# A state-space and SwiGLU kernel on one core: spectra stored in quarters of 64 channels, and some work of the chunk loop moved between engines

## The chip, the core and the metric

The kernel runs on one core of a Trainium2 chip. The core has TensorE for matmuls (PE, with its weight loads shown as PEld), VectorE (DVE), ScalarE (ACT), GpSimd (POOL) and SyncE (SP), which here only issues DMAs. All DMAs, whichever queue issued them, share 16 DMA engines. The metric is device microseconds of one execution; a kernel's time is the median of its runs.

## The reference

Two layers, each a state-space convolution and then a SwiGLU feed-forward block, both on a layer norm and with a residual. The sequence has 2048 steps, 512 channels (D) and 128 states per channel (N); the inner width is 1376.

```python
dt = jnp.exp(log_dt)[:, None]
logdA, dB = dt * (A_re + 1j * A_im), dt * (B_re + 1j * B_im)
P = jnp.exp(logdA[:, :, None] * l[None, None, :])
K = jnp.einsum("dn,dnl,dn->dl", Cc, P, dB).real        # a kernel of 2048 taps per channel
y = causal_convolution(u, K) + u * Dskip               # written with FFTs of length 4096
...
x = x + A(layernorm(x)); x = x + B(layernorm(x))       # twice, with the same weights
# B: (silu(x @ w_gate) * (x @ w_up)) @ w_down
```

So the work is: make K from the parameters, convolve, and do the feed-forward matmuls.

## The kernel before, in words

**The two parts.** The first part, to about 288 us, makes the kernel K and its spectra. The second, from about 360 us, runs the blocks of 512 steps (`ssm` for the convolution, `ffn` for the feed-forward), with a transition in between. In the second part Tile's scheduler orders the instructions; in the first the order on ScalarE, VectorE, TensorE and GpSimd is that of the program text (`manual_schedule`).

**Making K.** The 512 channels are cut into 8 chunks of 64 (`DC`). For a chunk, the 2048 taps are written as a product of two factors, 32 by 64 powers, per state and channel:
- `gen_turns` (L373) shifts and doubles phase angles on VectorE (L377 for the small tile xz, L380 and L384 for the large one) and clears one row with GpSimd (L386);
- `gen_trig` (L389) makes sines and cosines on ScalarE, first of xz (four activations of 320 elements a partition, L393 to L398), then of the large tile (three of 2048);
- `gen_exp` (L401) makes decays on ScalarE;
- `gen_e` (L426) and `gen_g` (L441) multiply these on VectorE to the factors re/im and g. At the last doubling of g (n = 16) the second half product goes to a tile acc (L461, L462), and a DMA on GpSimd's queue adds it into g (L463);
- `lags` (L476) is 128 small matmuls on TensorE that contract over the states.

**Spectra.** `spread_in` (L494) copies the lags' result to SBUF on ScalarE. `spread` (L497) writes that to DRAM (kdr) and reads it back in four DMAs (kt), which brings lags to partitions; both are issued by SP. `skip` (L487) adds the direct term Dskip into the first lag, on VectorE. `spectra` (L527) does 32 matmuls for two of the four frequency groups (q0 and q0 + 2), copies the results out of PSUM with four ScalarE activations (L544 to L546), stores half products to DRAM (wdr) from SP's queue and, when these have landed, adds the others to them with accumulating DMAs from GpSimd's queue (`store_w`, L524). wdr holds, for each half of the channels and each frequency group, 128 partitions of two parts (real, imaginary) of 256 channels; a chunk writes 64 channels of each part, 256 bytes in a row.

**Norms of the weights.** `norms` (L302) runs beside: GpSimd's queue loads blocks of the feed-forward weights (tiles st, three buffers), ScalarE squares them (L321), TensorE sums the squares (L324), VectorE takes the largest (L327). Three blocks make a group here. `second_block` adds 8 matmuls a part for the second block of the input (L287).

**The order.** Each step is entered in a list with a planned time (`at`), relative to the start t of its chunk (`starts`: 0, 31, 62, 93, then 28 apart); the list is sorted and the text runs in that order. The times have no other meaning: each engine does its instructions in this order and waits for what each needs. Around the change, in a chunk's turn: lags at t; `upper`, the square L417, at t + 0.2; the factors' first steps from t + 0.2; the copy L494 and the spread at t + 7.1; squares of a first group of weights at t + 8.0 and loads of the second at t + 8.1; decays from t + 8.3; the half product and its DMA at t + 12.2; turns of the chunk after next at t + 13.0; squares of the second group at t + 14.5; sines at t + 17.0; the direct term at t + 17.1; spectra at t + 17.5 (the first two groups) and in the next turn at 6.9 (the other two).

In the second part, for each frequency group VectorE multiplies input spectra u with w (L756), sums (L759) and combines the parts (L760, L761); u and w come from w0r in SBUF or from wdr and udr in DRAM.

Of the kernel before, what the change touches and what calls it, by code (L numbers as in the profile page):

```python
# [16 lines left out]
OP = mybir.AluOpType  # L17
# [18 lines left out]
NCH = D // DC  # L36
NA = 5
# [36 lines left out]
def kernel(ctx, tc, x, a_re, a_im, b_re, b_im, c_re, c_im, log_dt, d_skip,  # L74
# [48 lines left out]
    w0r = sb.tile([P, 2, 4, 2, HD], F32, name="w0r")  # L123
# [19 lines left out]
    wdr = dram.tile([NB, 2, 4, P, 2, HD], F32, name="wdr")  # L143
    udr = [dram.tile([NB - 1, 2, 4, P, 2, HD], F32, name=f"udr{i}") for i in range(NL)]
# [89 lines left out]

    def norm_x(n):
        rs, nb = row_stats(n, 4, 1.0, "stats", lambda r: tl([P, D], "junk", "t1", BF16))
        for c in range(4):
            A.activation(n[:, c], n[:, c], AF.Identity, scale=rs[:, c:c + 1], bias=nb[:, c:c + 1])

    def forward(n, h, eh):  # L240
# [13 lines left out]
        for i, q in enumerate(QORD):  # L254
# [9 lines left out]
            with tc.high_priority(offset=BOOST):  # L264
# [7 lines left out]
                u = tl([P, 2, HD], "u", "u")  # L272
                A.activation(u, pf, AF.Copy, scale=2.0 ** -16 if eh else 1.0)  # L273
# [7 lines left out]
    def direct(b, h, q, n, space=psml):  # L281
# [7 lines left out]
        u = tl([P, 2, HD], "u", "uu")  # L289
        A.activation(u, pf, AF.Copy)  # L290
# [82 lines left out]
    def gen_turns(ch, ts):  # L373
# [4 lines left out]
                        am.unsqueeze(2).to_broadcast([P, 5, DC]), OP.logical_shift_left)  # L378
        tu = im[:, 33:65].bitcast(I32)
# [61 lines left out]
    def gen_g(ch, ts, g):  # L441
# [12 lines left out]
        for n in (1, 2, 4, 8, 16):  # L454
# [5 lines left out]
            if n == 16 and 0 < ch < NCH - 1:  # L460
                tmp = tl([P, 2, 16, DC], "acc", ("gb", "ga")[ch % 2])  # L461
# [25 lines left out]
    def skip(ch, kt):  # L487

        k = kt[0:1, :, 0]
        V.tensor_tensor(k, k, dsk[:, ch * DC:(ch + 1) * DC].rearrange("p (g d) -> p g d", g=4), OP.add)  # L490
# [33 lines left out]
    def store_w(h, off, q, wo, eng=nc.sync, **add):  # L524
        eng.dma_start(wdr[1:, h, q, :, :, off:off + DC].rearrange("k p i d -> p i k d"), wo.rearrange("p i k g d -> p i k (g d)"), **add)

    def spectra(ch, kt, q0):  # L527


        h, off = ch // 4, (ch % 4) * DC  # L530
# [4 lines left out]
        if q0:  # L535
            wo = spare[0][:, 16 * DC:].rearrange("p (j i k g d) -> p j i k g d", j=2, i=2, k=NB - 1, g=4)
        else:
            wo = tl([P, 2, 2, NB - 1, 4, 16], "wo", "sg")
        wf = pw.rearrange("p j i k g d -> p j i k (g d)")
        wa = tl([P, 2, 2, NB - 1, 4, 16], "wa", "z")  # L540
        wv = wo.rearrange("p j i k g d -> p j i (k g d)")
        pv = pw.rearrange("p j i k g d -> p j i (k g d)")
        for i, sign in signs(q0):
            A.activation(wv[:, :, i], pv[:, :, 1 - i, :3 * DC], AF.Copy, scale=sign)  # L544
        A.activation(wa.rearrange("p j i k g d -> p j i (k g d)"), pv[:, :, :, DC:], AF.Copy)
# [695 lines left out]
```

## Time and profile before

| what | us |
|---|---|
| median of three runs | 1205.04 (1196.44 to 1207.28) |
| the profiled execution, its own time | 1204.58 |
| its span, first to last instruction | 1202.8 |
| set-up, to the first copy L494 at 69.30 | 69.3 |
| chunk loop, 69.30 to 288.21 | 218.9 |
| transition, to 360 | 71.8 |

A line of a profile's table gives where it stands: start and length for single instructions, or a group's busy time, mean and the idle time just before it with what ended that idle time. `[3.12 <-DMA kt<-kdr]` says: the engine had stood idle 3.12 us, and the last thing that it waited for was the DMA that fills kt from kdr. xN at the end of a row is a number of instructions. In the table by stretches (two times joined by a colon) each engine has its busy time and its number of instructions, and the last three columns are the granted clock of TensorE, the mean busy share of the DMA engines and GB/s.

### The profile page before, as it was taken

Reading aid. Unit: us, or ns where it says so; the run is one execution under the profiler, and the core shown is the slowest. Engines: PE = TensorE matmul, PEld = TensorE weight load, DVE = VectorE, ACT = ScalarE, POOL = GpSimd, SP = SyncE. Lnnn points to the kernel's source line nnn. Section 1 sums busy time; section 2 is a strip of 40 time slices with the busy share of each in tenths; the row PEclk is TensorE's granted clock in tenths of the full one; section 3 lists DMA queues with packets and bytes.
Section 4 is the critical chain, followed back from the end, with each engine's and each line's share of the span. In section 5 each row is a group of like instructions: output and inputs, shape, how many; then the busy total and the mean of one; then the engine's idle time right before and its main releaser. Section 6 shows DMA issues by size and latency. Waiting matters only on the chain.

```text
span 1202.8 us, 24436 instructions
## 1 busy us (share of the span) xinstructions
PE 1110.1 (92%) x9948; PEld 882.1 (73%) x9948; DVE 996.9 (83%) x1586; ACT 594.9 (49%) x1193; POOL 133.0 (11%) x176
## 2 busy tenths in 40 slices
PE   1978888998799999999999999999999998999998
PEld 1767777787687676878777686868687685867875
DVE  7998879685978999999899999999997999973211
ACT  6678777743283345356744253664533452234211
POOL 0013323332000010001110000010200000000000
PEclk9989999989999999999999999999999999999999
DMA  5368889989566337443324444342545145302000
GB/s 201 128 158 156 181 172 179 174 192 202 188 217 186 108 116 202 128 131 86 101 89 146 132 145 155 105 122 94 139 121 189 45 119 158 111 23 45 14 23 18
DMA packets 156915, 156.28 MB, mean 130 GB/s; under 512 B 95857, under 2 KB 104049, under 8 KB 156802
## 3 DMA queue, kind: packets, MB, share of 16 engines
q1 hardware_dynamic: 129314, 126.47, 35.0%
q0 software_dynamic: 27488, 28.25, 12.6%
q8 instruction: 78, 1.28, 0.4%
q14 instruction: 35, 0.29, 0.1%
HBM read 101.85 MB, written 36.57 MB: 115 GB/s over the span
## 4 chain that ended last, share of the span: by engine, by line
PE 33%; DVE 27%; issue 5%; DMA 4%; ACT 2%; SPq 1%; POOL 1%; DVEq 0%; POOLq 0%; ACTq 0%
PE pgu L888 6%; PE pgu L889 6%; PE pgu L891 6%; DVE t L756 5%; DVE yk L759 4%; PE py L903 3%; PE py L904 3%; PE py L905 3%; DMA mix<-nn 3%; DVE yk L756 2%; PE pi L775 2%; PE pf L271 2%; DVE z L227 2%; DVE hl L897 1%; DVE sg L895 1%
## 5 line engine op out<-in xcount | busy, mean ns | idle before, releaser
L888 PE MATMUL pgu<-mix,wsl 128*128 128x256 f16 x1280 | 298.9, 273 | 6.6 <-DVE xf L908 3.1
L889 PE MATMUL pgu<-mix,wsl 128*128 128x256 f16 x1280 | 298.8, 273 | 0.0
L891 PE MATMUL pgu<-mix,wsl 128*128 128x256 f16 x1280 | 193.9, 273 | 0.0
L889 PEld LDWEIGHTS <-wsl 128*128 128x128 f16 x1280 | 125.2, 98 | 23.6 <-issue 7.8
L903 PE MATMUL py<-wsl,hh 128*128 128x512 f16 (+1 forms) x352 | 134.1, 381 | 7.6 <-DVE xf L908 4.2
L888 PEld LDWEIGHTS <-wsl 128*128 128x128 f16 x1280 | 125.2, 98 | 15.9
L891 PEld LDWEIGHTS <-wsl 128*128 128x128 f16 x1280 | 125.3, 98 | 14.7
L905 PE MATMUL py<-wsl,hl 128*128 128x512 f16 (+1 forms) x352 | 133.9, 380 | 0.0
L904 PE MATMUL py<-wsl,hh 128*128 128x512 f16 x320 | 121.8, 381 | 0.0
L756 DVE TENSOR_TENSOR t<-uu,w 128x1024 f32<-128x1024 f32 x96 | 117.6, 1225 | 4.1 <-DMA w<-wdr 3.8
L759 DVE TENSOR_TENSOR yk<-yk,t 128x1024 f32<-128x1024 f32 x96 | 117.5, 1224 | 0.3
L895 DVE SCALAR_TENSOR_TENSOR sg<-pgu,sc,sg 128x512 f32<-128x512 f32 x80 | 60.2, 753 | 48.8 <-ACT sg L894 48.7
L518 PE MATMUL pw<-kt,ek 128*128 128x256 f32 (+1 forms) x384 | 99.2, 399 | 0.0
L894 ACT ACTIVATE sg<-pgu,sc 128x512 f32<-128x512 f32 x80 | 54.4, 681 | 84.4 <-PE pgu L891 80.2
L896 ACT ACTIVATE hh<-sg 128x512 f16<-128x512 f32 x80 | 50.1, 626 | 79.7 <-DVE sg L895 79.4
L518 PEld LDWEIGHTS pw<-kt,ek 128*128 128x128 f32 x384 | 79.0, 210 | 11.1
L775 PE MATMUL pi<-yl,mix 128*128 128x256 f16 x576 | 79.0, 272 | 4.6 <-DVE yl L227 2.7
L271 PE MATMUL pf<-z,eh 128*128 128x256 f16 x576 | 74.2, 273 | 1.5 <-DVE z L227 1.5
L756 DVE TENSOR_TENSOR yk<-u,w0r 128x1024 f32<-128x1024 f32 x56 | 68.7, 1226 | 1.4 <-ACT u L273 1.3
L904 PEld LDWEIGHTS <-hh 128*128 128x128 f16 (+1 forms) x352 | 34.6, 98 | 44.1 <-issue 9.1
L775 PEld LDWEIGHTS <-mix 128*128 128x128 f16 x576 | 56.1, 98 | 14.1 <-issue 3.4
L897 DVE TENSOR_TENSOR hl<-sg,hh 128x512 f16<-128x512 f32 x80 | 55.4, 693 | 12.8 <-ACT hh L896 12.7
(235 smaller groups left out, 2190.5 us busy)
## 6 DMA issues: line engine op xcount, KB each, us to landing
w<-wdr SPq DMA_DIRECT2D x96, 256.0 KB, 2.7
uu<-udr SPq DMA_DIRECT2D x96, 256.0 KB, 3.0
udr<-u POOLq DMA_DIRECT2D x32, 256.0 KB, 2.7
g<-acc POOLq DMA_DIRECT2D x6, 1024.0 KB, 9.1
wdr<-wa POOLq DMA_DIRECT2D x26, 192.0 KB, 5.4
udr<-u SPq DMA_DIRECT2D x16, 256.0 KB, 2.8
n<-ndr SPq DMA_DIRECT2D x16, 256.0 KB, 5.1
n<-xdr SPq DMA_DIRECT2D x4, 1024.0 KB, 5.7
```

The source lines that it names most:

```text
L271: PE.matmul(pf[:, o], lhsT=e, rhs=m, start=k == 0, stop=k == len(terms) - 1)
L518: PE.matmul(pw[:, i], lhsT=e, rhs=kt[:, :, c + 4 * k0:4 * k1:4, :].rearrange("p g k d -> p k g d"), start=c == 0, stop=c == 3)
L756: V.tensor_tensor(t, uu.unsqueeze(1).to_broadcast([P, 2, 2, HD]), w.unsqueeze(2).to_broadcast([P, 2, 2, HD]), OP.mult)
L759: V.tensor_tensor(yk, yk, t, OP.add)
L775: PE.matmul(pi[:, o], lhsT=e, rhs=m, start=k == 0, stop=k == len(terms) - 1)
L888: PE.matmul(o, lhsT=wgu(wi, k, 0)[:, fs], rhs=nh[:, k], start=k == 0, stop=False)
L889: PE.matmul(o, lhsT=wgu(wi, k, 1)[:, fs], rhs=nh[:, k], start=False, stop=False)
L891: PE.matmul(o, lhsT=wgu(wi, k, 0)[:, fs], rhs=nlo[:, k], start=False, stop=k == 3)
L895: V.scalar_tensor_tensor(sg, pgu[:, 1], sc6[:, 4:5], sg, OP.mult, OP.mult)
L903: PE.matmul(py[:, r], lhsT=hh[:n, f, rc], rhs=wd(f, 0)[:n], start=f == 0, stop=False)
L904: PE.matmul(py[:, r], lhsT=hh[:n, f, rc], rhs=wd(f, 1)[:n], start=False, stop=False)
L905: PE.matmul(py[:, r], lhsT=hl[:n, f, rc], rhs=wd(f, 0)[:n], start=False, stop=f == FT - 1)
```

## The change

- w0r, wdr and udr, and the tiles that go with them, hold quarters of 64 channels with both parts side by side: of a half's 256 channels, part by part before, now [quarter, part, 64]. A chunk's row in wdr is 512 bytes. ScalarE writes this order when it copies out of PSUM (`parted`, `whole` are views), with five activations a spectrum in place of four, and the products' operands and the combination read it.
- `skip` takes its engine; in the chunk loop this is GpSimd, at t + 12.5. The last chunk's stays on VectorE.
- The tile of g for the chunk after the next is taken early (t + 8.05), and the half product goes to its upper halves instead of to a tile acc.
- `gen_turns` is cut after L377; that step goes to t + 0.35 and the sines of xz to t + 0.45 (both of the chunk two ahead). The tiles are taken at t + 0.05.
- The first group's loads go from t - 1.4 to t - 13.0 and its squares from t + 8.0 to t + 0.25; the second group's loads go from t + 8.1 to t + 0.3.

```diff
-    w0r = sb.tile([P, 2, 4, 2, HD], F32, name="w0r")
+    w0r = sb.tile([P, 2, 4, NQ, 2, DC], F32, name="w0r")          # NQ = HD // DC = 4
-    wdr = dram.tile([NB, 2, 4, P, 2, HD], F32, name="wdr")
+    wdr = dram.tile([NB, 2, 4, P, NQ, 2, DC], F32, name="wdr")
...
+    def parted(t):
+        return t.rearrange("p c i d -> p i c d")
+    def whole(t):
+        return t.rearrange("p i (c d) -> p i c d", c=NQ)
...
-                u = tl([P, 2, HD], "u", "u")
-                A.activation(u, pf, AF.Copy, scale=2.0 ** -16 if eh else 1.0)
+                u = tl([P, NQ, 2, DC], "u", "u")
+                A.activation(parted(u), whole(pf), AF.Copy, scale=2.0 ** -16 if eh else 1.0)
...
                         am.unsqueeze(2).to_broadcast([P, 5, DC]), OP.logical_shift_left)
+        yield
         tu = im[:, 33:65].bitcast(I32)
...
             if n == 16 and 0 < ch < NCH - 1:
-                tmp = tl([P, 2, 16, DC], "acc", ("gb", "ga")[ch % 2])
+                tmp = gs[ch + 1][:, :, 16:32]
...
-    def skip(ch, kt):
+    def skip(ch, kt, eng):
         k = kt[0:1, :, 0]
-        V.tensor_tensor(k, k, dsk[:, ch * DC:(ch + 1) * DC].rearrange("p (g d) -> p g d", g=4), OP.add)
+        eng.tensor_tensor(k, k, dsk[:, ch * DC:(ch + 1) * DC].rearrange("p (g d) -> p g d", g=4), OP.add)
...
-    def store_w(h, off, q, wo, eng=nc.sync, **add):
-        eng.dma_start(wdr[1:, h, q, :, :, off:off + DC].rearrange("k p i d -> p i k d"), wo.rearrange("p i k g d -> p i k (g d)"), **add)
+    def store_w(h, c, q, wo, eng=nc.sync, **add):
+        eng.dma_start(wdr[1:, h, q, :, c].rearrange("k p i d -> p k (i d)"), wo.rearrange("p k i d -> p k (i d)"), **add)
...
         for i, sign in signs(q0):
-            A.activation(wv[:, :, i], pv[:, :, 1 - i, :3 * DC], AF.Copy, scale=sign)
-        A.activation(wa.rearrange("p j i k g d -> p j i (k g d)"), pv[:, :, :, DC:], AF.Copy)
-        A.activation(w0r[:, h, q0::2, :, off:off + DC], wf[:, :, :, 0], AF.Copy)
+            A.activation(wo[:, :, :, i], pv[:, 1 - i, :, :NB - 1], AF.Copy, scale=sign)
+        for i in range(2):
+            A.activation(wa[:, :, :, i], pv[:, i, :, 1:], AF.Copy)
+        A.activation(w0r[:, h, q0::2, cq], pw[:, :, :, 0].rearrange("p j i g d -> p j i (g d)"), AF.Copy)
...
-                V.tensor_tensor(t, uu.unsqueeze(1).to_broadcast([P, 2, 2, HD]),
-                                w.unsqueeze(2).to_broadcast([P, 2, 2, HD]), OP.mult)
+                V.tensor_tensor(t, uu.unsqueeze(2).to_broadcast([P, NQ, 2, 2, DC]),
+                                w.unsqueeze(3).to_broadcast([P, NQ, 2, 2, DC]), OP.mult)
...
-            at(t + 0.4, tiles)
+            at(t + 0.05, tiles)
...
+            at(t + 0.35, steps["turns"])
+            at(t + 0.45, tr)
             at(t + 13.0, steps["turns"], 6)
-            at(t + 17.0, tr, 2)
+            at(t + 17.0, tr)
...
-            at(t + 0.1, tiles)
+            if c == 1:
+                at(t + 0.1, lambda: tiles(c))
+            if c + 1 < NCH:
+                at(t + 8.05, lambda: tiles(c + 1))
...
-            at(t + (17.1 if c < NCH - 2 else 12.5), lambda: skip(c, kt))
+            at(t + 12.5, lambda: skip(c, kt, G))
...
-            for k, t0, t1, t2, t3 in ((0, -1.4, 8.0, 13.9, 22.3), (1, 8.1, 14.5, 17.45, 22.9),
+            for k, t0, t1, t2, t3 in ((0, -13.0, 0.25, 13.9, 22.3), (1, 0.3, 14.5, 17.45, 22.9),
```

`later_parts`, `first_parts`, `direct`, `inputs` and the tiles wo, wa, w, uu, t and yk take the new order in the same way.

More of the change, by code (lines that the diff above doesn't have):

```diff
@@ L288, in direct @@
         yield
-        u = tl([P, 2, HD], "u", "uu")
-        A.activation(u, pf, AF.Copy)
+        u = tl([P, NQ, 2, DC], "u", "uu")
+        A.activation(parted(u), whole(pf), AF.Copy)
         nc.sync.dma_start(udr[0][b, h, q], u)
```

68 lines of the change are left out of this document (35 added, 33 removed).

## The prediction

> **What bounds the kernel now.** I read the page first, then busy time by stage, then the stage of the change engine by engine, and last what each queue waits for.
>
> ```profile
> span 1202.8 us, 24436 instructions
> ...
> PE 1110.1 (92%) x9948; PEld 882.1 (73%) x9948; DVE 996.9 (83%) x1586; ACT 594.9 (49%) x1193; POOL 133.0 (11%) x176
> ```
>
> ```profile
> 360.00:1202.00 842.00, 814.61 (x6782) 626.89 (x6779) 701.48 (x1159) 355.82 (x688) 50.45 (x68) 1.00 0.37 109
> ```
>
> The columns are the stretch, its length, busy time of PE, PEld, DVE, ACT and POOL, the granted clock, the DMA share and GB/s. From 360 us on TensorE is busy 814.61 of 842.00 us at clock 1.00: that part is bound by matmuls, which the change leaves alone. The part to study is the chunk loop. I cut it at the starts of the copy L494, which follows each chunk's lag products; a stretch between two of them is called a round, 0 to 6.
>
> ```profile
> 69.30:98.78 29.48, 22.73 (x311) 18.49 (x311) 28.95 (x34) 22.70 (x51) 8.01 (x11) 0.88 0.70 169
> 98.78:131.30 32.52, 29.23 (x343) 24.90 (x343) 29.07 (x34) 25.88 (x55) 11.72 (x14) 0.95 0.88 176
> 131.30:163.45 32.15, 29.03 (x343) 24.89 (x343) 26.47 (x32) 24.87 (x55) 10.96 (x13) 0.89 0.89 173
> 163.45:195.16 31.71, 28.46 (x342) 24.81 (x343) 25.05 (x32) 24.88 (x54) 10.98 (x13) 0.95 0.86 167
> 195.16:226.17 31.01, 27.07 (x342) 23.55 (x342) 27.36 (x34) 24.48 (x54) 10.79 (x13) 0.94 0.88 173
> 226.17:259.96 33.79, 29.66 (x343) 25.55 (x343) 26.80 (x32) 25.21 (x56) 12.52 (x14) 0.90 0.98 186
> 259.96:288.21 28.25, 28.17 (x378) 23.84 (x379) 15.35 (x15) 11.02 (x23) 7.80 (x10) 1.00 0.85 197
> ```
>
> Rounds 0 to 5 last 29.48 + 32.52 + 32.15 + 31.71 + 31.01 + 33.79 = 190.66 us. VectorE works 28.95 + 29.07 + 26.47 + 25.05 + 27.36 + 26.80 = 163.70 us of it, so it idles 26.96. No engine is full, the DMA engines are near 0.9, and the clock is below 1: a loop of waits sets the period. Round 2 on TensorE shows it:
>
> ```profile
> 131.11 0.70 PE L518 MATMUL pw<-kt,ef 128*128 128x256 f32 x2
> ...
> 138.12 0.60 PE L324 MATMUL nrm<-sq,onesb 128*128 128x344 bf16 x3
> ...
> 142.01 0.71 PE L324 MATMUL nrm<-sq,onesb 128*128 128x344 bf16 x3
> 145.85 1.19 PE L518 MATMUL pw<-kt,ef 128*128 128x256 f32 x2 [3.12 <-DMA kt<-kdr]
> ...
> 155.77 0.45 PE L483 MATMUL pk<-re,g 128*32 128x64 f32 x8
> ```
>
> ```profile
> L518 PE MATMUL pw<-kt,ef 128*128 128x256 f32 (+1 forms) x121 | 41.1, 424 | 20.9 <-DMA kt<-kdr 13.7 <-DVE re L438 3.9 <-DVE kt L490 3.3
> ```
>
> TensorE runs out of work at 142.72, waits 3.12 us for the spread kernel kt, and then does 32 matmuls in 155.77 - 145.85 = 9.92 us that took 138.12 - 131.11 = 7.01 us just before: the gap costs 3.1 us and the clock after it 2.9. All such gaps sum to 20.9 us, six rounds' worth. The next lags stand behind these matmuls, so the loop is: lags, copy, spread through DRAM, spectra, lags.
>
> VectorE waits for the same transfer, since it does the direct term, and once more for the cosine:
>
> ```profile
> L490 DVE TENSOR_TENSOR kt<-kt,tdk 1x64 f32<-1x64 f32 x8 | 1.7, 211 | 29.4 <-DMA kt<-kdr 15.7 <-ACT kt L512 13.7
> ...
> L449 DVE TENSOR_TENSOR g<-w,re 128x128 f32<-128x128 f32 x8 | 2.3, 285 | 7.9 <-ACT re L398 7.9
> ```
>
> Where the transfer's time goes, by the two issuing queues:
>
> ```profile
> 132.35 0.33 SPq L501 DMA_DIRECT2D kdr<-ks  x1
> 135.69 2.61 SPq L503 DMA_DIRECT2D kt<-kdr  x4
> ```
>
> ```profile
> 127.88 3.31 POOL L525 DMA_DIRECT2D wdr<-wa  x2 [7.95 <-DMA wdr<-wo]
> 133.00 1.71 POOL L315 DMA_DIRECT2D st<-in_B_w_gate_dram  x3 [1.81 <-ACT sq L321]
> ...
> 135.06 1.25 POOL L463 DMA_DIRECT2D g<-acc  x1 [0.19 <-issue]
> ```
>
> ```profile
> 128.00:130.00 2.00, 2.00 (x74) 2.00 (x70) 1.97 (x2) 0.00 (x0) 2.00 (x2) 1.00 0.03 8
> ...
> 134.00:136.00 2.00, 2.00 (x11) 1.75 (x10) 1.93 (x5) 1.99 (x10) 1.81 (x5) 1.00 0.93 284
> ...
> 148.00:150.00 2.00, 2.00 (x6) 1.55 (x6) 0.45 (x1) 2.00 (x2) 2.00 (x5) 0.50 1.03 82
> ```
>
> From the copy's store to kt pass 145.85 - 132.35 = 13.5 us. In that stretch lie two accumulating wdr stores, three weight loads and the accumulate of g, while the DMA engines stood empty from 128 to 130 (share 0.03). At 148, when little but wdr accumulates in 256-byte runs moves, a share of 1.03 carries only 82 GB/s, against 284 at 0.93.
>
> **The change, part by part.**
>
> ```profile
> st<-in_B_w_gate_dram POOLq DMA_DIRECT2D x16, 172.0 KB, 6.1
> ```
>
> *Weight loads and squares moved.* The second group's loads (3 x 172 KB by this row) go from behind the first squares (133.00) to plan time t + 0.3, before the lags end. 516 KB at 284 GB/s is 1.8 us that leaves the spread's way, if the empty stretch takes them; bounds 0 (they are still moving when kdr starts) and 1.8. I take 1.8, for 128 to 130 holds next to nothing. On GpSimd they now stand ahead of the pair of accumulates (127.88), which is issued up to 1.7 us later; what waits for it is the next copy into the tile wa, half a round on: 0. The first group's loads go from behind one accumulate to before it; their tiles are released by the squares at t + 14.5, when kt is nearly in: nothing, the old place being as busy.
>
> *Runs of 512 bytes.* Every wdr store and accumulate has 384 runs instead of 768. A pair of accumulates is 2 x 128 x 6 x 256 bytes, 393 KB, at 82 GB/s 4.8 us of all DMA engines; the pair issued at 127.88 moves while the spread begins. The least gain is nothing (cost by the byte), the most half, 2.4 us (cost by the run). I take two thirds of the way, 1.6, since 82 against 284 GB/s says that the run counts.
>
> The Trainium skill (DMA: Bandwidth & Descriptors, Specifications) says that a transfer needs at least 512 B to run at line rate and is otherwise read, modified and written. By that rule I would take the upper bound, 2.4 us; the 82 GB/s agrees, and no row here shows the 512-byte form.
>
> So kt comes 1.8 + 1.6 = 3.4 us earlier (0 to 4.2). TensorE needs 3.1, and has no gap then; without gaps the slow clock goes too. That alone would free 20.9 us of gaps and up to 2.9 us a round of clock, more than VectorE allows.
>
> *Direct term on GpSimd.*
>
> ```profile
> 140.63 0.21 DVE L490 TENSOR_TENSOR kt<-kt,tdk 1x64 f32<-1x64 f32 x1 [2.50 <-DMA kt<-kdr]
> ```
>
> ```profile
> L205 POOL TENSOR_TENSOR rs<-rs,mhalf 128x4 f32<-128x4 f32 (+1 forms) x3 | 3.4, 1127 | 72.9 <-DVE rs L204 72.9
> ```
>
> VectorE loses seven of the eight adds (0.21 us each) and their wait, 15.7 us over four rounds. On GpSimd it stands behind L463 (135.06 + 1.25 = 136.3) and waits for the first of four kt transfers. Behind it wait the zero of im, the next weight loads and an accumulate, none due before the next lags. The price of one such add is not in the trace: least 0.21 (L490), most 1.13, the power in the second row. I take 1.13, hidden: L490 ended at 140.84 in round 2, 5.0 us before TensorE had all of kt; if that cover goes, it costs 6 x 1.13 = 6.8.
>
> *Sines and squares on ScalarE.* These rows are round 2:
>
> ```profile
> 151.60 2.29 DVE L431 TENSOR_TENSOR im<-im,re 128x2048 f32<-128x2048 f32 x1
> ```
>
> ```profile
> 131.30 1.02 ACT L494 ACTIVATE ks<-pk 128x1024 f32<-128x1024 f32 x1 [4.34 <-PE pk L484]
> 132.22 1.24 ACT L321 ACTIVATE sq<-st 128x344 bf16<-128x344 f32 x3
> ...
> 143.68 0.47 ACT L393 ACTIVATE xz<-xz 128x320 f32<-128x320 int32 x1
> ...
> 145.37 1.90 ACT L396 ACTIVATE re<-im 128x2048 f32<-128x2048 int32 x1
> ...
> 149.18 1.99 ACT L398 ACTIVATE re<-re,hpi 128x2048 f32<-128x2048 f32 x1
> ...
> 163.45 1.02 ACT L494 ACTIVATE ks<-pk 128x1024 f32<-128x1024 f32 x1 [3.87 <-PE pk L484]
> ```
>
> ScalarE is full from 131.30 to 151.17. The squares (1.24) and the four small activations (145.37 - 143.68 = 1.69) leave this stretch and go to where it waited 3.87 us for the lags: L398 ends 2.9 us earlier and L449's wait (7.9 in all) goes. Their input L377 moves with them, to behind L431 (ended 153.89), early enough for 163.45. Table loads stay two a round, nothing between the big sines and the new place asking for another table. If the lags come sooner, the 3.87 shrinks, and what does not fit delays L494; 3.87 - 2.93 leaves 0.9.
>
> *Half products.* L462 writes into the tile of g two chunks on, the same buffer as before. What may not be overwritten, the lags' operand, is the same: 0. The accumulate lands a round before that half is written.
>
> *Layout in spectra and products.* One more activation a spectrum, 13 in all: two of 384 elements for one of 768.
>
> ```profile
> L545 ACT ACTIVATE wa<-pw 128x768 f32<-128x768 f32 x13 | 11.2, 858 | 2.1 <-DMA wdr<-wa 2.1
> ...
> L544 ACT ACTIVATE wo<-pw 128x384 f32<-128x384 f32 x14 | 6.4, 514 | 16.9 <-PE pw L518 16.9
> ```
>
> That is 2 x 514 - 858 = 170 ns each, 13 x 0.17 = 2.2 us on an engine with idle time: 0; without that cover, 2.2. The 152 products read runs of 64 with a repeat in between. L459 has that pattern already, beside it a plain sum:
>
> ```profile
> L459 DVE TENSOR_TENSOR g<-g,xz 128x1024 f32<-128x1024 f32 x8 | 9.9, 1232 | 0.3
> ```
>
> ```profile
> L759 DVE TENSOR_TENSOR yk<-yk,t 128x1024 f32<-128x1024 f32 x96 | 117.5, 1224 | 0.3
> ```
>
> The difference, 8 ns, times 152 is 1.2 us, beside TensorE work: 0, bounds -1 and +2.
>
> **The sum.** TensorE's loop would give more than 21 us, so VectorE is late next. Its idle 26.96 plus six adds, 1.3, is the most that can go: 28.2. I leave 8 of it as waits, about 1.3 us a round, because L462 must still wait for the lags and L449 for ScalarE. That is -20; round 6 is bound by TensorE (28.17 of 28.25) and its kernel does not go through DRAM: 0. The profiled execution took 1204.58 us (0.46 under the median of 1205.04): 1204.58 - 20 = 1184.6, say 1184.
>
> **The rivals.**
>
> 1. *Nothing moves.* The loads and the accumulate only queue up ahead of kdr instead of behind it, and runs of 512 cost by the byte. For: DMA shares of 0.86 to 0.98 in rounds 1 to 5. Against: the empty 128 to 130. Then the skip and sine moves only shift VectorE's waits to L462: about 1203.
>
> 2. *Half.* Kt comes 1.5 us sooner, the gap shrinks to 1.6 and the clock still falls: 6 x 1.5 = 9, about 1195.
>
> The Trainium skill (TensorE: Matmul & The Clock Gate, What's actually happening) has the clock halved after an idle window of about 3.4 us; the 0.50 at 148 after a 3.12 us gap agrees, and by it a gap of 1.6 would cost no clock, which brings this rival to VectorE's limit, the forecast's 1184.
>
> 3. *Slower.* The loads stand ahead of the accumulate on GpSimd and both ahead of kdr. If all 516 KB move inside the kdr store at round 2's mean of 173 GB/s, kdr and with it every lag is 3.0 us later, with no slack on TensorE: 6 x 3.0 = 18, about 1222. It decides once the delay of kdr exceeds what kt gains behind it. Against: the loads are issued some 3 us before the copy.
>
> 4. *The add holds VectorE.* GpSimd's add and VectorE's products shut each other out; 6 x 1.13 = 6.8: about 1191. For and against no row: L386's zero merely ran beside VectorE. The Trainium skill (SBUF — State Buffer, Who interferes with whom) says that a VectorE instruction with two SBUF inputs and a GpSimd one that reads SBUF exclude each other for a whole instruction; by that rule this rival holds, at 0.2 to 1.1 us an add.
>
> **How the numbers follow.** Forecast 0.68 (its own range 1176, the whole 28.2, to 1192), half 0.13, nothing 0.10, slower 0.05, add 0.04. One per cent, 12 us, is about what a measurement of this kernel can tell from no change; the border is 1193. Faster: 0.68 + half of 0.13 + most of 0.04 = 0.77. Slower: 0.05 and a little of "nothing", 0.07. Same: 0.16. The range runs from 1174 (2 us below the floor, for the tail's stores) to 1203, leaving the slower rival out.
>
> **What would show it.** Right: no wait of L518 for kt above 1 us, clock 0.98 or more in rounds 1 to 5, rounds of 28 to 29 us, L449 without its wait, L525 on POOL at about 1 us instead of 1.65 each, L759 and L756 still near 1.23. Wrong: kt still 13 us behind L494, or VectorE waiting at L462 for the lags in every round; the add on POOL ending after the last kt transfer; anything past 360 us longer by more than 3 us.

## The result, and the profile after

The changed kernel takes 1200.13 us (median of 20 runs, 1196.37 to 1205.52), the kernel before 1200.99 (20 runs, 1190.27 to 1209.67): ratio 1.0003 [0.9981, 1.0024], no difference that can be measured. 1184 was forecast, so the gain of 20 us did not come. The profiled execution took 1196.63 us, near the fastest of its kernel, and that of before 1204.58, above the median of these 20: the 8 us between the two profiles are no result. Here and below a median is over all executions, while a ratio leaves out those more than 1.5 per cent above the fastest of their own kernel: one of e3's four (1196.3), one of e12's eight, two of e15's six, four of e17's ten, and of the kernel before 11 of the 29 beside e13 to e16 and 5 of the 13 beside e17 and e18.

The page of the changed kernel, then the same two DMA lines of the page before:

```profile
span 1194.8 us, 24454 instructions
PE 1109.1 (93%) x9948; PEld 880.3 (74%) x9948; DVE 995.7 (83%) x1579; ACT 600.0 (50%) x1208; POOL 132.7 (11%) x183
DMA packets 134643, 156.28 MB, mean 131 GB/s; under 512 B 51313, under 2 KB 81777, under 8 KB 134530
q0 software_dynamic: 17504, 28.25, 11.6%
```

```profile
DMA packets 156915, 156.28 MB, mean 130 GB/s; under 512 B 95857, under 2 KB 104049, under 8 KB 156802
q0 software_dynamic: 27488, 28.25, 12.6%
```

The parts of the change are there: over a third fewer packets on GpSimd's queue (q0), seven adds fewer on VectorE, more instructions on GpSimd. The same cut as in the prediction, at the starts of the copy of ks (now L504):

```profile
68.33:96.00 27.67, 22.21 (x313) 18.10 (x313) 27.16 (x33) 23.84 (x52) 5.81 (x11) 0.88 0.61 159
96.00:124.03 28.03, 28.03 (x348) 24.70 (x347) 27.58 (x33) 25.83 (x59) 10.23 (x15) 1.00 0.90 200
124.03:157.09 33.06, 29.71 (x347) 25.21 (x346) 32.54 (x35) 24.70 (x59) 10.30 (x15) 0.90 0.81 168
157.09:188.52 31.43, 26.81 (x333) 23.03 (x332) 24.25 (x30) 25.17 (x57) 10.96 (x15) 0.94 0.83 177
188.52:220.26 31.74, 28.66 (x342) 24.67 (x343) 26.50 (x31) 24.61 (x56) 10.98 (x15) 0.89 0.88 180
220.26:252.37 32.11, 28.58 (x343) 24.88 (x344) 27.47 (x31) 23.83 (x53) 11.11 (x16) 0.95 0.87 186
252.37:282.06 29.69, 28.57 (x378) 24.05 (x379) 12.69 (x12) 10.02 (x21) 9.08 (x9) 1.00 0.81 181
```

Rounds 0 and 1 are as short as was forecast: 27.67 and 28.03 us, in round 1 with TensorE never idle and the clock at 1.00. From round 2 on the loop is as long as before. The forecast happened, and was lost in the middle of the loop. ScalarE's rows show where:

```profile
151.49 0.87 ACT L554 ACTIVATE wa<-pw 128x384 f32<-128x384 f32 x2 [8.23 <-DMA wdr<-wa]
...
157.09 1.00 ACT L504 ACTIVATE ks<-pk 128x1024 f32<-128x1024 f32 x1
```

ScalarE stands 8.23 us at the copy into wa, since the accumulating DMAs of the last spectrum still read that one tile. It then works without a pause up to the copy of ks, which therefore comes late. VectorE has had no such wait. GpSimd's queue shows what follows (L473 issues the accumulate of g, L535 those of wdr, L500 is the direct term; L390, which is named as the end of waits, is VectorE's next instruction after the half product), and TensorE's row the price:

```profile
104.17 1.19 POOL L473 DMA_DIRECT2D g<-g  x1 [6.07 <-DVE im L390]
...
131.10 1.19 POOL L473 DMA_DIRECT2D g<-g  x1 [4.70 <-DVE im L390]
...
140.91 1.30 POOL L535 DMA_DIRECT2D wdr<-wa  x1 [5.62 <-DMA wdr<-spare]
143.81 1.29 POOL L535 DMA_DIRECT2D wdr<-wa  x1 [1.60 <-DMA wdr<-spare]
...
157.88 2.33 POOL L473 DMA_DIRECT2D g<-g  x1
169.85 0.31 POOL L500 TENSOR_TENSOR kt<-kt,tdk 1x64 f32<-1x64 f32 x1 [9.64 <-DMA kt<-kdr]
...
191.11 1.20 POOL L473 DMA_DIRECT2D g<-g  x1 [1.64 <-DVE im L390]
...
222.85 1.19 POOL L473 DMA_DIRECT2D g<-g  x1 [0.92 <-DVE im L390]
```

```profile
171.41 1.19 PE L528 MATMUL pw<-kt,ef 128*128 128x256 f32 x2 [4.38 <-DMA kt<-kdr]
```

In rounds 1 and 2 the accumulate of g is issued 104.17 - 96.00 = 8.2 and 131.10 - 124.03 = 7.1 us after the copy of ks, when the spread is nearly through. In rounds 3 to 5 it is issued 0.8, 2.6 and 2.6 us after it, so its 1 MB goes out with the spread, and kt is late again: TensorE waits 4.38, 3.08 and 3.53 us there. How long one transfer of kt takes (KB, and median us from issue to landing), in round 1, in round 4, and in round 2 of the kernel before:

```profile
kt<-kdr SPq DMA_DIRECT2D x4, 128.0 KB, 2.9
```

```profile
kt<-kdr SPq DMA_DIRECT2D x4, 128.0 KB, 6.3
```

```profile
kt<-kdr SPq DMA_DIRECT2D x4, 128.0 KB, 8.2
```

So the loads of kt take twice the time when the accumulate of g moves beside them: 2.9 and 3.0 us in rounds 1 and 2, and 7.0, 6.3 and 7.4 in rounds 3 to 5. In the kernel before it went out ahead of them in each of rounds 1 to 5, by 0.2 to 1.6 us, and they took 5.0 to 8.2.

The late accumulates of wdr, for which the copy into wa waited, have a forerunner on SP's queue. In round 1 the stores wdr<-spare, to which the accumulates of wdr add, were issued 0.34 us ahead of the accumulate of g and landed after 2.6 us; in round 2 they were issued 0.75 us behind it and took 10.0 us, so the accumulates of wdr went out only at 140.91 and 143.81. No run changes this alone.

From the last copy of ks to the end of the span little changed: 1202.8 - 288.21 = 914.6 us before, 1194.8 - 282.06 = 912.7 after.

### The profile page after: what moved, and what is told of

Same layout as the page of the kernel before. It is cut to its first block, busy times and chain, and to the rows that moved or that the text cites. A ratio compares the mean times of both kernels' runs of the same rounds, so it can differ in the third digit from the quotient of the medians.

```text
span 1194.8 us, 24454 instructions
## 1 busy us (share of the span) xinstructions
PE 1109.1 (93%) x9948; PEld 880.3 (74%) x9948; DVE 995.7 (83%) x1579; ACT 600.0 (50%) x1208; POOL 132.7 (11%) x183
## 4 chain that ended last, share of the span: by engine, by line
PE 33%; DVE 22%; issue 9%; DMA 6%; POOL 1%; SPq 1%; ACT 1%; DVEq 0%; POOLq 0%; ACTq 0%
PE pgu L900 5%; PE pgu L901 5%; PE pgu L903 5%; DVE t L767 3%; PE py L915 3%; PE py L916 3%; PE py L917 3%; DVE yk L770 3%; PE pi L787 2%; DVE yk L767 2%; DMA mix<-nn 2%; DVE z L228 2%; PE pf L280 2%; DVE sg L907 1%; DMA w<-wdr 1%
## 5 line engine op out<-in xcount | busy, mean ns | idle before, releaser
L528 PE MATMUL pw<-kt,ek 128*128 128x256 f32 (+1 forms) x384 | 96.7, 391 | 0.0
L528 PEld LDWEIGHTS pw<-kt,ek 128*128 128x128 f32 x384 | 77.1, 205 | 10.5
L493 PE MATMUL pk<-re,g 128*32 128x64 f32 x1024 | 61.5, 301 | 5.5 <-DVE re L448 3.3
```

The costliest lines, as they stand in the source:

```text
L528: PE.matmul(pw[:, i], lhsT=e, rhs=kt[:, :, c + 4 * k0:4 * k1:4, :].rearrange("p g k d -> p k g d"), start=c == 0, stop=c == 3)
```

## The experiments

Three theories after the result, with the letters that some of the expectations use. **Order** (G): the accumulate of g now overtakes the spread. **Tile** (S): the single tile wa throws the loop into that order. **Capacity** (C): the DMA engines are full and the order is beside the point.

### e1_again: the changed kernel once more

> The changed kernel as it is, one more profiled execution. In the first one, rounds 0 and 1 took 27.7 and 28.0 us and rounds 2 to 5 took 31.4 to 33.1. If the switch has a cause in the program (the accumulate that reads the one tile wa ends too late and ScalarE waits for it, theory S), it comes again in the same place: two or three rounds under 29 us, then a wait of ScalarE of some 8 us at the copy into wa, then rounds over 31. If it is chance (rival), the fast rounds stand elsewhere or are missing.

1207.42 us. Its rounds are 29.25, 35.13, 30.58, 31.53, 31.93, 30.01 and 31.09 us: here the good order is lost in round 1 already, and ScalarE had not waited for wa before that. So the tile was not what started it in this execution, against the first expectation. In round 1 the accumulate left 6.61 us after the copy, but the store of kdr took 5.9 us to land (4.4 in the first execution), so that the loads of kt went out 0.39 us behind the accumulate, and TensorE waited 5.32 us. How many rounds go well differs between executions.

### e2_hold_g: the accumulate of g held back

```diff
-            at(t + 12.5, lambda: skip(c, kt, G))
+            at(t + 11.1, lambda: skip(c, kt, G))
```

GpSimd then stands at the direct term, which needs kt's first part, before it can issue the accumulate of g.

> The direct term goes ahead of the accumulate of g on GpSimd's queue, so that this 1 MB transfer is issued only when the first part of kt has landed. Theory G (what keeps the late rounds long is that the accumulate of g goes ahead of the spread's two steps): kt passes its wait about 10 us after the copy instead of 13.3, late rounds fall to 28 to 30 us, 1185 to 1193 us in all. Theory S alone (the single tile wa throws the loop back once, and the rest follows): little, 1196 to 1201. Theory C (the DMA engines are simply full, order does not matter): nothing, or up to 10 us worse since the lags then wait for the accumulate, 1200 to 1210.

1188.72 us (1188.14 to 1190.95), ratio 0.9859 [0.981, 0.9908].

```profile
134.13 2.00 POOL L500 TENSOR_TENSOR kt<-kt,tdk 1x64 f32<-1x64 f32 x1 [6.06 <-DMA kt<-kdr]
136.09 0.76 POOL L473 DMA_DIRECT2D g<-g  x1
```

```profile
ACT wa L554 <- DMA wdr<-wa: 26.4, 6, 6.7
PE pw L528 <- DMA kt<-kdr: 0.5, 2, 0.3
```

The accumulate leaves 136.09 - 125.57 = 10.5 us after the copy, and TensorE's waits for kt sum to 0.5 us (us in total, times, longest). The order is a cause, and shown alone: one number in a list moved it, and the time fell as expected. ScalarE still waits 26.4 us for wa; in these rounds that does not lead to a wait for kt, but they last 28.5 to 31.4 us.

### e3_wa2: a second place for wa

```diff
-        wa = tl([P, 2, NB - 1, 2, DC], "wa", "z")
+        wa = tl([P, 2, NB - 1, 2, DC], "wa", "nn" if q0 else "z")
...
-            at(t + 25.0, lambda: sizes(c, kt, box["ks"]))
+            at(t + 25.0, lambda: sizes(c, kt, kt2[:, (c + 1) % 2]))
```

> A second place for the half products wa: those of the second two frequency groups go to the buffer of ks, and the junk output of the sizes goes to the other half of kt2. Theory S: ScalarE does not wait at wa, rounds stay under 29 us to the end of the loop, 1183 to 1190. Theory G alone: the wait goes, but the accumulate of g gets ahead of kt anyway in some round, 1195 to 1200. Theory C: 1198 to 1202.

1182.86 us (1177.05 to 1196.26), ratio 0.9791 [0.9721, 0.9861]. No wait for wa is left. The profiled execution is the slowest of the four: three rounds of 28.1 to 28.2, then the accumulate came 5.0 us after a copy, 0.6 us ahead of the loads of kt, and that round and the next two took 30.5 to 32. So the tile is a cause too, by the ratio of three executions, but without the hold the good order is not safe.

### e4_moves_only and e6_layout_only: the change cut in two

e4 has the moves (direct term, sines, squares, loads, half products) in the layout of before; e6 has the new layout and none of the moves.

> The kernel before with all that the change moves (loads, squares, sines, direct term on GpSimd, half product's tile) but with the old layout in 256-byte runs. If the layout gives back what the moves cost, this is slower than the kernel before, 1205 to 1215; if the 512-byte runs are worth little (their packets halved, but the accumulates' queue only fell from 12.6 to 11.6 per cent of the span), it is the changed kernel's time, 1197 to 1203.

> The new layout alone, all moves undone. If the prediction's step on the 512-byte runs holds (1.6 us of every spread), some 5 us faster than the kernel before. If accumulates cost by the byte, as their queue's share suggests (12.6 per cent of the span before, 11.6 after), nothing: within 4 us of the kernel before.

e4: 1201.75, ratio 0.9957 [0.9932, 0.9981]. e6: 1193.81 (1187.72 to 1201.31), ratio 0.992 [0.9884, 0.9956]. e4 came out as was expected if the runs are worth little, but e6 did not: the layout alone and the moves alone each gain a little, and the two together (1.0003) nothing. So some move takes the layout's gain back.

### e5_hold_wa2: hold and second tile together

> Both cures: the accumulate of g behind the direct term on GpSimd, and a second place for wa. If each takes away one of two separate causes (holding removed the long rounds but left 26 us of ScalarE's waits at wa; the second wa removed those waits but the loop still fell back in one execution), all rounds take 27 to 29 us in every execution: 1176 to 1182, with executions within 4 us of each other. If the two are one and the same cause (rival), no better than the second wa's good executions or the holding alone: 1183 to 1189.

1182.65 us (1179.91 to 1184.43), ratio 0.9825 [0.9769, 0.9882]: faster than both kernels, and the executions differ by 4.5 us only. The time falls between the two expectations, and the intervals of e2, e3 and e5 overlap, so whether order and tile are two causes or one stays open.

```profile
67.89:95.67 27.78, 23.69 (x318) 19.64 (x317) 27.27 (x33) 23.83 (x52) 6.46 (x11) 0.88 0.60 160
95.67:122.68 27.01, 26.40 (x337) 22.60 (x336) 26.56 (x32) 25.87 (x58) 10.62 (x16) 1.00 0.96 211
122.68:148.86 26.18, 25.79 (x343) 22.83 (x343) 25.73 (x31) 25.00 (x57) 9.86 (x14) 1.00 0.96 210
148.86:176.01 27.15, 27.12 (x342) 23.98 (x342) 26.70 (x32) 25.28 (x56) 10.86 (x15) 1.00 0.94 202
176.01:205.14 29.13, 26.19 (x342) 22.76 (x342) 28.65 (x34) 24.60 (x57) 11.61 (x16) 0.98 0.90 200
205.14:233.86 28.72, 28.44 (x343) 24.90 (x344) 26.02 (x30) 23.64 (x53) 11.80 (x15) 0.96 0.93 203
```

The same engines, the same work, and in rounds 1 to 3 200 to 211 GB/s at shares of 0.94 to 0.96, where the changed kernel moved 168 to 186 from round 2 on. Capacity is not what ended the gain.

### e7_loads_back and e8_moves_hold

e7 is the changed kernel with the weights' loads and squares at their old times; e8 is e4 with the hold, so the old layout in the good order.

> The changed kernel with the weight loads and their squares back at their old times. If the earlier loads matter for the fast rounds 0 and 1 (the prediction's 1.8 us of every spread, 2.9 with the squares on ScalarE), rounds 0 and 1 take 29 and 32 us again and the time is that of the kernel before or up to 5 us more. If the loads in their new place are what fills the DMA engines behind kt and makes the accumulates late (rival), the wait at wa goes and the time falls, 1190 to 1196.

> As in the held version (direct term ahead of the accumulate of g), but with the old layout in 256-byte runs. It measures the layout where the order is no longer the limit. If runs of 512 bytes save DMA time that counts, this is slower than the held version with the new layout (1188.7) by 4 us or more; if accumulates cost by the byte, the same within 3 us.

e7: 1198.25, ratio 0.9962 [0.9922, 1.0002]; not told from the whole. Neither expectation held: rounds 0 and 1 took 26.1 and 28.1 us, and ScalarE still waited for wa (5.78 us). e8: 1196.38, ratio 0.9942 [0.9914, 0.997], against 0.9859 [0.981, 0.9908] for e2, which differs from it in the layout alone. Where the order is held, runs of 512 bytes are worth 1196.38 - 1188.72 = 7.7 us, or 0.83 per cent by the ratios, though the two were timed on different chips. Against e4 (0.9957 [0.9932, 0.9981]), from which it differs in the hold alone, e8 is not faster by what can be told: TensorE waits no more for kt, but ScalarE waits 5.9 to 6.2 us for wa in each of rounds 2 to 5, and rounds 2 to 5 take 29.9 to 31.7 us. In the old layout the hold alone moves the wait and gains nothing that shows.

### e9_skip_back, e10_sines_back: single moves undone

e9 puts the direct term back on VectorE at t + 17.1, e10 the sines and turns at their old times; all else is as changed.

> The changed kernel with one move undone: the direct term is added by VectorE again, between its waits, where the kernel before has it. Layout, sines, squares, weight loads and half products stay as changed. Theory (the direct term on VectorE is the brake that keeps the accumulate of g behind the spread): VectorE waits again for the first part of kt in each round, so L473's accumulate is issued 3 to 8 us after the start of the copy of ks instead of 0.8 to 2.6, kt comes without a gap in more rounds, and the time falls from 1200 to the 1193.8 of the layout alone or a little below: ratio 0.988 to 0.994. Rival (another of the moves takes the layout's gain back, the direct term has no part in it): 1197 to 1203, ratio 0.996 to 1.002, with L473 still issued within 3 us of the copy from round 2 on. Rival (the direct term costs VectorE its time and its wait for kt, as the prediction had it): slower than the whole change, over 1203.

> The changed kernel with the sines and turns at their old times; direct term on GpSimd, layout, squares, weight loads and half products as changed. If the sines' move takes the layout's gain back (ScalarE has them between the spectra's copies, and the copies of pw and of ks come later): 1192 to 1196, ratio 0.988 to 0.994. If only the direct term does: no change from the whole, 1198 to 1203, ratio 0.997 to 1.003, and ScalarE still waits about 8 us at the copy of wa in one round, after which L473's accumulate leaves within 3 us of the copy of ks.

e9: 1207.23, ratio 1.0018 [0.9984, 1.0052]. The theory is wrong: with VectorE waiting for kt again, the accumulate still leaves 1.3 and 2.6 us after two of the copies. Taking the direct term from VectorE is not what did the harm. (1207 lies in the range of the last expectation, but the kernel before took 1206.65 on this chip, and the ratio is not apart from that of the whole.) e10: 1200.41, ratio 0.9952 [0.993, 0.9975], between the two expectations. In both, and in e7, the good order ends as in the changed kernel, with the wait for wa. ScalarE's row of each and the next accumulate on GpSimd, e9 first, then e10:

```profile
125.04 0.87 ACT L554 ACTIVATE wa<-pw 128x384 f32<-128x384 f32 x2 [8.16 <-DMA wdr<-wa]
130.64 1.00 ACT L504 ACTIVATE ks<-pk 128x1024 f32<-128x1024 f32 x1
```

```profile
131.97 2.30 POOL L473 DMA_DIRECT2D g<-g  x1
```

```profile
122.77 0.87 ACT L553 ACTIVATE wa<-pw 128x384 f32<-128x384 f32 x2 [5.04 <-DMA wdr<-wa]
126.67 1.03 ACT L503 ACTIVATE ks<-pk 128x1024 f32<-128x1024 f32 x1
```

```profile
130.98 1.19 POOL L472 DMA_DIRECT2D g<-g  x1
```

### e11_best_loads_back, e12_layout_wa2

e11 is e5 with the loads and squares at their old times; e12 is e6 with the second tile.

> The version with both cures (the direct term at t+11.1 on GpSimd, ahead of L473, and a second place for wa), which measured 1182.7, with the squares' weight loads at their old times. If the earlier loads are of use where the spread has no gap to fill: slower than 1182.7 by up to 0.5 us in each round, 1183 to 1187. If they only press on the same DMA engines while those are full (e7 was 2 us below the whole change with them back): 1178 to 1182. Nothing is left of kt's gap in either, PE's wait for kt under 1 us in all.

> The layout alone, with a second place for wa and none of the moves (direct term on VectorE, sines, squares, loads and half products as in the kernel before). Theory (two causes, the order of L473's accumulate and the single wa; the moves shorten a round only once neither throws it back): the waits of ScalarE for wa are gone, the direct term on VectorE holds the accumulate, and the rounds come to about 29 to 30 us: 1184 to 1191, ratio 0.982 to 0.990, above the 1182.7 of the version with the moves and both cures. Rival (wa's wait is a symptom, the moves are what makes rounds 28 us): 1191 to 1196, ratio 0.990 to 0.995, as the layout alone. Rival (the moves are worth nothing even then): 1180 to 1184.

e11: 1184.59 (1182.99 to 1187.66), ratio 0.9832 [0.9792, 0.9872]. Its time is in the first range, its ratio not apart from that of e5 (0.9825): where the order holds, the earlier loads are worth nothing that these runs can tell. e12: 1194.97 (1182.58 to 1201.4), ratio 0.9895 [0.9855, 0.9935]; the interval spans two of the expectations, so it decides little.

### e13 to e16: which move takes the layout's gain, on one chip

e13 is the whole change, e14 the layout alone. e15 is the whole with sines, turns, loads and squares at their old times (direct term and half products as changed); e16 is its counterpart, the layout with only sines, turns, loads and squares moved.

> The changed kernel as it is, timed beside the three below on one chip and against the kernel before. It gives the base for them: 1198 to 1204 is expected, ratio 0.996 to 1.002.

> The layout alone again, beside the whole on one chip. If the moves take back what the layout gives (layout alone measured 0.992, the whole 1.0003, on different chips): 1191 to 1197, at least 4 us below the whole. If the difference of the two was one of chips: within 3 us of the whole.

> The changed kernel with sines, turns and the squares' weight loads at their old times; direct term on GpSimd, layout and half products as changed. If the earlier sines and loads are what takes the layout's gain back (each undone alone came to about 0.996): 1191 to 1196, as the layout alone, ScalarE waiting for wa less than 3.5 us at a time. If it is the direct term on GpSimd with the half products: as the whole, within 3 us.

> The layout with sines, turns and the squares' weight loads as changed; the direct term on VectorE and the half products in a tile of their own as in the kernel before. If the earlier sines and loads take the layout's gain back: as the whole or above it, 1198 to 1207 (with the half products also as changed, 1207 was measured). If the half products' tile does, because it lets the next factors and with them L473's accumulate go ahead: 1191 to 1196, as the layout alone.

| kernel | median us | ratio |
|---|---|---|
| e13, whole | 1202.22 | 0.9996 [0.9963, 1.0028] |
| e14, layout | 1199.43 | 0.9951 [0.9916, 0.9985] |
| e15, without early sines and loads | 1195.03 | 0.9873 [0.9825, 0.9921] |
| e16, early sines and loads alone | 1208.25 | 1.0042 [1.0007, 1.0077] |

The early sines and loads take the gain: e16 is apart from e14, e15 from the whole. The means over all executions say the same: e16 is 9.8 us above e14, e15 7.6 below e13. The layout alone is 2.8 us below the whole by the medians, less than the 4 expected, and their intervals overlap here. The direct term on GpSimd and the half products do no harm (e15 is no slower than e14).

### e17_wa2_no_early, e18_all_cures: by the same way or a third one?

e17 is e15 with the second tile, e18 has the hold as well.

> Layout, direct term on GpSimd and half products as changed, sines, turns and the squares' weight loads at their old times, and a second place for wa. If the two causes add (the early sines and loads bring L473's accumulate to 2.6 us behind the copy; the single wa makes the copy late): 1178 to 1184, ratio 0.977 to 0.985, and steadier than the second place for wa alone, which measured 1177 to 1196. If the second place takes the gain alone: about the same 1183, with the same spread.

> The same with the direct term at t+11.1 as well, so that L473's accumulate can't be issued before the first part of kt has landed. If the hold already does all that the later sines and loads do: 1181 to 1186, as the version with both cures and the early sines (1182.7), PE's wait for kt under 1 us. If the later sines also spare ScalarE's copies of pw: 1177 to 1181.

e17: 1184.69, ratio 0.9867 [0.9817, 0.9918], in two clusters: six executions from 1176.5 to 1184.9, four from 1195.2 to 1200.8. So it is no steadier than e3, and that expectation fell. Nor is it apart from e15 (0.9873), which has one place for wa. e18: 1184.27 (1179.53 to 1188.68), ratio 0.988 [0.9789, 0.997], like e5 and e11. Once the accumulate is held and wa has two places, early or late sines and loads make no difference that shows. That fits their having acted through the same two causes.

**All rounds together.** I put side by side rounds 1 to 5 of the 15 profiled executions without the hold (before, after, e1, e3, e4, e6, e7, e9, e10, e12 to e17): how long after the copy of ks the accumulate of g is issued, and whether TensorE then waits at the spectra, for kt or for what GpSimd and VectorE do behind it.

| accumulate of g issued | rounds | TensorE waits 1.5 us or more | median wait |
|---|---|---|---|
| under 5.5 us after the copy | 46 | 46 | 3.6 us |
| 5.5 us or later | 29 | 6 | 0.4 us |

The 5.5 us stand for the issue of kt's loads, which comes, behind the store of kdr, 3.8 to 7.3 us after the copy. In 45 rounds the accumulate of g is issued ahead of them, and TensorE waits 1.5 us or more in all 45; in 30 it is issued behind them, and TensorE does so in 7, in six of which it is behind by less than 0.8 us.

In six of these executions ScalarE waited 5.0 to 8.4 us for wa within rounds 0 to 4, and each time the next accumulate left 0.8 to 4.3 us after the copy. In the other nine it was lost after shorter waits for wa or none, or was never good (the kernel before).

## Why the prediction was wrong, step by step

**The bound and the loop: right in the main.** Past the loop little changed, and in the kernel before the loop is set by the spread through DRAM: where kt comes in time and wa has two places, rounds 1 to 5 take 26 to 29 us in e5 (26 to 31 in e18). With kt in time and one place for wa they take 28.5 to 31.4 (e2), which points to the tile as a second limit that the prediction did not have.

**Kt 3.4 us earlier, so no gap and no slow clock in six rounds: this is the step that failed.** For kt it held in rounds 1 and 2; in round 0 TensorE still waited 2.00 us, and in rounds 3 to 5 3.08 to 4.38. The prediction put the lateness of kt down to the weight loads (1.8) and the runs of 256 bytes (1.6). What the runs show in their place is the accumulate of g: issued ahead of the loads of kt it makes them land after 6.3 to 7.4 us instead of 2.9 to 3.0, and held behind them it leaves TensorE waits for kt of 0.5 us in all (e2). The working took this accumulate as fixed in its place in round 2. But it is released by VectorE and the spread by ScalarE's copy, so their order is the outcome of a race. The prediction made VectorE earlier and let ScalarE be late without a price.

**Sines and squares.** The row L449 was to lose its wait of 7.9 us; it did not (it is L459 now; us in total, times, longest):

```profile
DVE g L459 <- ACT re L408: 9.4, 2, 5.2
```

The larger mistake is in the sentence that L462 must still wait for the lags, which I counted only as idle time of VectorE. Behind that half product stands the issue of 1 MB. VectorE in round 4 of the changed kernel (copy of ks at 188.52):

```profile
188.52 2.29 DVE L472 TENSOR_TENSOR g<-g,xz 128x2048 f32<-128x2048 f32 x1 [1.23 <-PE pk L494]
```

VectorE stands ready when the lags end, so the accumulate leaves 2.6 us after the copy, as early as the lags allow: twice in the changed kernel, four times in e1, twice in e13. That is a gain on VectorE, paid for in the spread. In the kernel before it left 3.4 to 6.1 us after the copy in rounds 1 to 5, which was too early already, since the loads of kt went out behind it each time.

**Weight loads.** 1.8 us a round were forecast. With the loads back the time did not change by what can be told (e7; e11 against e5). As far as these runs tell, the empty stretch at 128 to 130 us was no room that something waited for. What I overlooked stands in the rows that I quoted: at 133.00 the loads wait for the squares, and L463 behind them goes out at 135.06 having waited for nothing but its issue. In that round the loads were a brake on the accumulate. In e15, where they are back, one L472 again starts directly behind them, 3.5 us after the copy:

```profile
218.33 1.75 POOL L324 DMA_DIRECT2D st<-in_B_w_up_dram  x3 [1.04 <-ACT sq L330]
220.03 0.21 POOL L418 MEMSET re<- 128x64 f32 x1
220.11 1.33 POOL L472 DMA_DIRECT2D g<-g  x1
```

How sines and loads share in the harm stays open: undone singly, each came out between the layout alone and the whole (e7 0.9962, e10 0.9952).

**Runs of 512 bytes.** 1.6 us a round were forecast, some 10 in all. The layout alone measured 0.992 [0.9884, 0.9956] and 0.9951 [0.9916, 0.9985], the pair e2 and e8 7.7 us, that is 6 to 10 us: the size was about right. The mechanism (cost by the run) is not what the traces show. With the layout alone GpSimd's queue takes 11.5% of the DMA engines' time instead of 12.6%, and the accumulates of wdr land after 5.5 us instead of 5.4.

```profile
q0 software_dynamic: 17504, 28.25, 11.5%
...
wdr<-wa POOLq DMA_DIRECT2D x26, 192.0 KB, 5.5
```

The 82 GB/s at 148 to 150 of the kernel before, at a share of 1.03, have a counterpart in runs of 512 bytes: in e3 at 170 to 172, where likewise nothing but GpSimd's queue moves, it is 96 GB/s at 1.07. By these two a pair of accumulates of 393 KB takes 4.8 and 4.1 us, an estimate of 0.7 us gained and not 1.6. The 82 was a low reading besides: the stretch begins empty, and in its second microsecond 113 to 164 GB/s move (82 to 195 in e3). GpSimd issues each of these accumulates in 1.3 us instead of 1.65, where about 1 was expected. The rule of the Trainium skill (DMA: Bandwidth & Descriptors, Specifications), by which transfers under 512 B do not run at line rate, was taken in the prediction as the upper bound, 2.4 us; by this trace 512 bytes help a little, and do not bring these accumulates to line rate. By what path the layout's 6 to 10 us come stays open.

**Direct term on GpSimd.** An add takes 857 ns in the mean there, where 1.13 us was taken, and is mostly hidden: TensorE's waits of 2.00 us in round 0 and 3.08 us in round 4 ended with it or with the zero of im behind it. What counts is its place in the queue: ahead of the accumulate (e2) or behind it.

```profile
L500 POOL TENSOR_TENSOR kt<-kt,tdk 1x64 f32<-1x64 f32 x7 | 6.0, 857 | 37.0 <-DMA kt<-kdr 27.6 <-ACT kt L522 9.3
```

"Behind it wait the zero of im, the next weight loads and an accumulate, none due before the next lags" was wrong in part: they were late in the rounds in which kt was late.

**The tile wa.** The row L545 stood in the prediction with 2.1 us of waits for DMA wdr<-wa in the whole execution, read only for its duration, and the prediction put the next copy into wa at 0, "half a round on". In the changed kernel one such wait took 8.23 us.

**Half products and layout in the products: right.** The 152 products and their sums cost what they did:

```profile
L767 DVE TENSOR_TENSOR t<-uu,w 128x1024 f32<-128x1024 f32 x96 | 117.1, 1220 | 4.9 <-DMA w<-wdr 4.2
L770 DVE TENSOR_TENSOR yk<-yk,t 128x1024 f32<-128x1024 f32 x96 | 117.1, 1220 | 0.2
```

**The sum.** VectorE's limit of 28.2 us less 8 was a fair size for what the parts can bring: with the order held and two places for wa it came, 1182.65 us at a ratio of 0.9825. That this is so near the 1184 forecast is partly luck, since e5 has two cures that the forecast did not have. The rival "nothing moves" came nearest, by another way than it gave: what moved came back as a late kt. The rival "slower" had the store of kdr late behind the loads; it is issued 125.05 - 124.03 = 1.0 us after the copy in round 2, as before (132.35 - 131.30), and lands after 4.2 to 4.8 us in rounds 1 to 5, where 3.3 to 5.2 were taken before. In the rival of the add that holds VectorE the wrong side pays: it is the add that waits for VectorE (the last section has the rows), and e15, which has it on GpSimd, is no slower than e14.

```profile
125.05 0.33 SPq L511 DMA_DIRECT2D kdr<-ks  x1
```

## What to carry to other kernels

When a change makes one engine earlier, list the large transfers that this engine releases and ask whose way they now get into: an early DMA of low urgency can cost more than the engine gained. Where two queues race for the same DMA engines, fix the order by a dependence of the urgent one's result (here the direct term ahead of the accumulate, one number in the order), not by planned times. A single buffer with a small wait in the profile before is a place to price at its worst, since a loop that depends on a race can be thrown over by one late instruction and stay so for the rest of the loop.

## What the runs showed of the hardware

- An accumulate of 1 MB from SBUF to SBUF takes 9.8 us to land in the changed kernel, and a transfer of kt beside it 6.3 us instead of 2.9, though it is on another queue and of 128 KB:

```profile
g<-g POOLq DMA_DIRECT2D x6, 1024.0 KB, 9.8
```

- How long TensorE waits does not alone say whether the slow clock follows. After a wait of 2.86 us that ended at 168.51 (e15) the clock stays at 1.00; after one of 2.17 us that ended at 109.74 (e13) it falls to 0.50, as after 4.38 us (the changed kernel); stretches of 2 us in this order:

```profile
169.00:171.00 2.00, 2.00 (x11) 1.75 (x10) 0.00 (x0) 1.97 (x3) 1.49 (x2) 1.00 0.01 2
```

```profile
112.00:114.00 2.00, 2.00 (x7) 1.55 (x6) 2.00 (x3) 2.00 (x3) 0.00 (x0) 0.50 0.91 299
```

```profile
172.00:174.00 2.00, 2.00 (x6) 1.62 (x5) 0.38 (x2) 2.00 (x3) 2.00 (x3) 0.50 0.73 242
```

  The Trainium skill (TensorE: Matmul & The Clock Gate, What's actually happening) gives an idle window of about 3.4 us; here a wait of 2.17 us was enough once, as were the 3.12 us in the kernel before, while the 2.86 us in e15 cost no clock.
- GpSimd's add of 64 elements takes between 0.31 and 1.86 us in the changed kernel, against 0.21 on VectorE. It waits for VectorE: the two adds that began while VectorE stood idle took 0.31 us, and the other five each ended 0.17 us after the VectorE instruction that was running when they began. One of them, VectorE's row first (it ends at 202.28, the add at 202.46, and VectorE's next instruction began at 202.21, not held up):

```profile
200.07 2.21 DVE L445 SCALAR_TENSOR_TENSOR im<-im,mu 128x1984 f32<-128x1984 f32 x1
```

```profile
200.89 1.57 POOL L500 TENSOR_TENSOR kt<-kt,tdk 1x64 f32<-1x64 f32 x1 [8.58 <-DMA kt<-kdr]
```

- What starts the late order in the executions of e3 and e17 that have two places for wa and lose it all the same stays open.
